# Key and value summaries of two groups of heads in one run of products, with the second group's keys and values in other buffers

## The chip, the cores and the metric

The kernel runs on one core of one Trainium2 chip. The metric is the device time of one execution in microseconds (us), as the median of several runs; lower is better. The kernel before was run three times: 836.36, 836.88 and 843.17 us.

## The reference

A small attention block feeds a gated feed-forward layer, and that feeds a layer of eight experts of which each token uses two. All of it is float32.

```python
batch, n_heads, seq, head_dim, n_mem = 4, 8, 576, 64, 32
a = exp(phi - max(phi, axis=2)); a = a / (sum(a, axis=2) + 1e-9)      # over the sequence
k_m = einsum('bhsm,bhsd->bhmd', a, k)                                 # key summary
v_m = einsum('bhsm,bhsd->bhmd', a, v)                                 # value summary
attn = softmax(q @ k_m.T / sqrt(head_dim)); x = attn @ v_m            # 2304 tokens x 512
y = (silu(x @ w_gate) * (x @ w_val)) @ w_out                          # d_ff = 1536
# experts: noisy top 2 of 8, h = relu(y @ w1[e]), out += weight * (h @ w2[e]), d_ff = 1024
```

The change touches the lines of `k_m` and `v_m` alone: for each of 4 batches and 8 heads, 32 memory rows of 64 columns, summed over 576 positions.

## The kernel before

**Stages.** The 2304 tokens are eight blocks of 288, two to a batch. The program is one list of instructions for each engine, in an order written out by hand. Stage `i` is the feed-forward layer of block `i`: 12 slots `f`, in each of which `gv(i, f)` issues 6 products into bank `pg` (line 473) and 6 into `pv`, `gate_act` makes the gated product on VectorE (DVE, lines 486 and 487), and `down` issues the output products `acc` of slot `f - 2` (line 502 in block 0, 506 later). Behind the eight stages come the experts (lines 987 to 1190).

**What is done beside a stage.** All else of the first half of the program stands at places inside the slots: `put(i, n, fn)` sets `fn` at half-slot `n` of stage `i` (n = 2f is the start of slot f, n = 2f + 1.5 lies between `gate_act` and `down`, n = 2f + 1.99 behind `down`), and `later(i, n, fn)` does so with n counted on into the next stage from 24. The table `AT["s1"]` holds these places for the summaries of batch 1 (row 1) and of batches 2 and 3 (row 2), counted from stage 2b - 2.

**The summaries.** The 8 heads of a batch are two groups `g` of 4. For a group, `s1_b` transposes the exponentials of `phi` on TensorE (PE, lines 288 to 291), `s1_bc` copies them to the tile `en`, and `s1_c` (line 310) issues 20 products into a bank `pkv`: 5 chunks of the sequence by 4 heads, each head in its own 32 columns of the array; the first 4 chunks have 128 rows, the last has 64. k and v stand side by side, so one product has 2 x 64 columns. `s1_cv` (line 319) scales the bank by the sum's reciprocal into `kz[g]` on VectorE, `s1_d` (line 328) transposes `kz[g]`, and `s1_dc` (line 336) copies the result to `KM[b]` on ScalarE (ACT). Group 1's `kz[1]` has a half of zeros (set once by GpSimd, POOL) so that its transposed rows land in the upper 64 partitions. The two groups run one behind the other, each at its own places.

**Buffers.** k and v of a batch (`load_kv`, issued by the SP queue) use one buffer `kv` for both groups in batches 1 to 3, so that group 1 is loaded only when group 0's products have read it; everything queued behind that load on SP waits with it. Three buffers of 1024 words with the tag `home` hold weights in block 0 (`stx`, from `wa`) and, at the start of the experts, the first weights `wf` and their low halves `wl`. PSUM banks 6 and 7 go round in turn to all that asks through `other`. One large store, `out<-zt`, which clears the output, is issued in stage 1 ahead of group 1's load of batch 2.

Of the kernel before, what the change touches and what calls it, by code (L numbers as in the profile page):

```python
# [7 lines left out]
F32 = mybir.dt.float32  # L8
# [4 lines left out]
I32 = mybir.dt.int32  # L13
U32 = mybir.dt.uint32
AF = mybir.ActivationFunctionType
# [5 lines left out]
B, H, S, D, M = 4, 8, 576, 64, 32  # L21
T = B * S
DM = 512
# [20 lines left out]
        7: (1.5, 4, 5, 4.05, 5.05, 6, 3, 6.05, 3.1, 3.5, 3.6, 3.7, 4, 4.01, 5.2, 6.1, 7.1, 7.2, 7.6, 7.7, 9.5, 9.6),  # L44
    },
    "s1": {
        1: (23.6, 24.02, 24.03, 25.9, 26, 26.9, 27, 27.8, 28, 27.9, 29, 31, 31.9, 33, 33.9),
        2: (9, 9.92, 13.2, 13.9, 15, 17.9, 19, 19.9, 21, 21.9, 23, 23.9, 25, 25.9, 27),
    },
# [20 lines left out]
def r(ap):  # L70
    return ap.bitcast(F32R)
# [3 lines left out]
def moe_program(ctx, tc, xin, wa, wgn, nz, wb, out):  # L75
# [10 lines left out]
    V, A, P, G, Q = nc.vector, nc.scalar, nc.tensor, nc.gpsimd, nc.sync  # L86

    const = ctx.enter_context(tc.tile_pool(name="const", bufs=1))
# [9 lines left out]
    def bank(n, shape, name):  # L98
        return psum.tile(shape, F32, tag=f"b{n}", name=name)
# [3 lines left out]
    def other(shape, name):  # L103
        spare.append(spare.pop(0))
        return bank(spare[-1], shape, name)
# [5 lines left out]
    gpool = right.enter_context(tc.tile_pool(name="gate", bufs=1, side="right"))  # L111
    att = left.enter_context(tc.tile_pool(name="att", bufs=1))


    PH, KV, QT, RA = {}, {}, {}, {}
    ROW = 18 * D

    def section(b, name):
        o, n = PLACE[name]
        return xin[b, o:o + 128 * n].rearrange("(p n) -> p n", n=n)  # L120

    def load_phi(b, g):
        t = att.tile([128, S], F32, tag="phi", name="phi", bufs=2)
        Q.dma_start(t, section(b, f"phi{g}"))
        PH[b, g] = t

    def load_part(b, g, s):
        if (b, g) not in KV:
            if b == 0 and g:
                KV[b, g] = wpool.tile([128, 4096], F32, tag="X1", name="kv", bufs=1)[:, :2 * ROW].rearrange(  # L130
                    "p (s w) -> p s w", s=2)
            else:
                KV[b, g] = att.tile([128, 2, ROW], F32, tag="kv", name="kv", bufs=1)
        Q.dma_start(KV[b, g][:, s], section(b, f"{'kv'[s]}{g}"))

    def load_kv(b, g):
        for s in range(2):
            load_part(b, g, s)
# [13 lines left out]
    for n in range(len(ORDER)):  # L152
        at, m = min((at, m) for at, m in freed if HOMES[m] is None or n < HOMES[m])
# [5 lines left out]
    def load_wa(n):  # L159


        m = HOME[n]
        if m < 4:
            RA[n] = gpool.tile([128, 1024], I32, tag="stg", name="stg", bufs=4)
        elif m < 8:
            if "x" not in RA:
                RA["x"] = wpool.tile([128, 4, 1024], I32, tag="X0", name="early", bufs=1)
            RA[n] = RA["x"][:, m - 4]
        else:
            if m not in RB:  # L170
                if m < 13:
                    RB[m] = wpool.tile([128, 1024], I32, tag="RW", name="stw", bufs=12)
                else:
                    RB[m] = gpool.tile([128, 1024], I32, tag="home", name="stx", bufs=3)
            RA[n] = RB[m]
        f, t = ORDER[n]
        Q.dma_start(RA[n].bitcast(I16)[:, :4 * DM - 1],
                    wa.bitcast(I16)[f][:, 4 * DM * t + 1:4 * DM * (t + 1)])

    RB = {}  # L180
# [4 lines left out]
    def ro_tile():  # L185
        return w1pool.tile([128, DM], F32, tag="RO", name="ro", bufs=12)
# [19 lines left out]
    def low(n):  # L206
# [5 lines left out]
        if n == 10:  # L212
            load_q(1)

    load_phi(0, 0)
    load_phi(0, 1)
    load_part(0, 0, 0)
    load_q(0)
    for g, s in ((1, 0), (0, 1), (1, 1)):
        load_part(0, g, s)  # L220
    for n in range(len(HOMES)):
# [7 lines left out]
    ident = const.tile([128, 128], F32, name="ident")  # L229
# [18 lines left out]
    e_cap = const.tile([128, E], F32, name="e_cap")  # L248
    G.iota(e_cap, pattern=[[T, E]], base=CAPS, channel_multiplier=0,
           allow_small_or_imprecise_dtypes=True)  # L250
    kz = [const.tile([128, 2, 1 + n, D], F32, name=f"kz{n}") for n in range(2)]
    G.memset(kz[1], 0.0)
    TOP = [w1pool.tile([128, 2 * DM], FP16, tag="OS", name="top", bufs=4) for _ in range(4)]
    for t in TOP:
        G.memset(t, 0.0)
# [4 lines left out]
    ST, KM = {}, {}  # L260
# [21 lines left out]
    TP = {}  # L282
# [17 lines left out]

    def s1_c(b, g, s=slice(0, 2)):

        en, st = ST[b, g]
        p = other([128, 2, D] if b else [128, D], "pkv")
        t = KV[b, g][:, s]
        for c in range(5):
            for h in range(4):
                o, d = (slice(0, 128), 4 * D * c + D * h) if c < 4 else (
                    slice(64 * (h // 2), 64 * (h // 2) + 64), 16 * D + D * (h % 2))
                P.matmul(p[32 * h:32 * h + 32], en[o, c, 32 * h:32 * h + 32], t[o, ..., d:d + D],  # L310
                         start=(c == 0), stop=(c == 4))
        TP[b, g, s if b == 0 else 2] = p

    def s1_cv(b, g, s=2, eng=None):
        st = ST[b, g][1]
        out = kz[g][:, :, g, :] if s == 2 else kz[g][:, s, g, :]
        p = TP.pop((b, g, s))
        if eng is None:
            V.tensor_scalar(out, p, st[:, 2:3], None, op0=OP.mult)
        else:  # L320
            A.activation(out, p, AF.Copy, scale=st[:, 2:3])

    def s1_d(b, g, s=2):

        p = other([128, 2, 128], "pT")
        for m in range(2):
            if s in (m, 2):
                P.transpose(p[:64 * g + 64, m, :], kz[g][:, m].rearrange("p n d -> p (n d)"), ident)
        TP[b, g, s] = p

    def s1_dc(b, g, s=2):
        if b not in KM:
            KM[b] = att.tile([128, 2, 4, M], F32, tag="km", name="km", bufs=2)
        o = slice(64 * g, 64 * g + 64)
        m = slice(0, 2) if s == 2 else slice(s, s + 1)
        A.activation(KM[b][o, m].rearrange("p s k m -> p s (k m)"), TP.pop((b, g, s))[o, m], AF.Copy)

    SM, X = {}, {}

# [105 lines left out]
    def os_tile():  # L445
        return w1pool.tile([128, DM], F32, tag="OS", name="os", bufs=4)
# [241 lines left out]
    def put(i, n, fn, *a):  # L688
        fill.setdefault((i, n), []).append((fn, a))
# [35 lines left out]
    def later(i, n, fn, *a):  # L725
        put(i + int(n // 24), n % 24, fn, *a)

    for b in range(1, B):
        i = 2 * b - 2
        n = AT["s1"][min(b, 2)]  # L730
        for g in range(2):
            later(i, 18.5 if b == 1 else -4, load_phi, b, g)
        later(i, 18.5 if b == 1 else -4, load_kv, b, 0)
        later(i, n[5] + 0.06, load_kv, b, 1)
        later(i, n[0], both, s1_a, b)
        later(i, n[1], both, s1_e, b)
        later(i, n[2], both, s1_r, b)
        for g in range(2):
            for m, fn in zip(n[3 + 6 * g:], (s1_b, s1_bc, s1_c, s1_cv, s1_d, s1_dc)):
                later(i, m, fn, b, g)  # L740
        for j, o in enumerate(AT["proj"][b]):
            i, f = 2 * b - 1 + o // NF1, o % NF1
            put(i, 2 * f + 1.95, proj_a, b, j)
            later(i, 2 * f + 2, proj_h, b, j)
            later(i, 2 * f + 2, proj_b, b, j)
    for i in range(1, NB):
        if i > 1:
            put(i - 1, 6, load_q, i)
        n = AT["s2"].get(i - 1, AT["s2"][2])
# [74 lines left out]
    WB, WH = {}, {}  # L824

    def load_wb(n):
        if n < len(STAGES) * NF2:
            if n < 2:
                WB[n] = gpool.tile([128, 1024], F32, tag="home", name="wf", bufs=3)
            elif "all" not in WB:  # L830
                WB["all"] = wpool.tile([128, 4, 1024], F32, tag="X1", name="wb", bufs=1)
            if n > 1:
                WB[n] = WB["all"][:, n % 4]
            Q.dma_start(WB[n], wb[STAGES[n // NF2], n % NF2])

    def prep2(n):
        if n % 2 == 0:
            tag = ("GH", "GL", "OS")[(n // 2) % 3]
            if n == 0:
                u = gpool.tile([128, 2, DM], F32, tag="home", name="wl", bufs=3)  # L840
                WH[n], WH[n + 1] = u[:, 0, :], u[:, 1, :]
            elif tag == "OS":
                WH[n], WH[n + 1] = os_tile(), os_tile()
            else:
                u = w1pool.tile([128, 2, DM], F32, tag=tag, name="wl", bufs=2)
                WH[n], WH[n + 1] = u[:, 0, :], u[:, 1, :]
        raw = WB[n]
        t = wpool.tile([128, 1024], F32, tag="RW", name="wm", bufs=12)
        u = ro_tile()
        A.activation(r(t), raw, AF.Copy)  # L850
        V.tensor_sub(r(u), raw[:, :512], t[:, :512])
        V.tensor_sub(r(WH[n]), raw[:, 512:], t[:, 512:])
        WB[n] = (t[:, :512], u, t[:, 512:], WH[n])
# [483 lines left out]
    for p in range(2):  # L1337
        for m in range(3):
            put(("u", (24, 25, 25, 28, 29, 29)[3 * p + m]), 1.2, sums_ws, p, m)
        for n in range(4):  # L1340
            u = (25, 26, 27, 27, 29, 30, 30, 31)[4 * p + n]
# [11 lines left out]
    for p in range(pairs):  # L1353
        e, q = 2 + p // 4, p % 4
        n = 24 + 2 * p
# [138 lines left out]
    with tc.If(full > 0), tc.tile_pool(name="last", bufs=1) as last:  # L1494
        w = last.tile([128, NF2, 1024], F32, name="wl")
# [58 lines left out]
```

## Time and profile before

| | |
|---|---|
| median of 3 runs | 836.88 us |
| the profiled execution, whole | 836.54 us |
| its span, first to last instruction | 834.7 us |
| PE busy | 820.9 us |
| DVE busy | 637.0 us |
| ACT busy | 391.8 us |
| POOL busy | 244.7 us |
| mean granted TensorE clock | 0.998 |

The profiled execution lies between the runs: 0.34 us under their median. The span leaves out 1.8 us around the first and the last instruction. Busy times overlap; PE's is nearly the span, but its matmuls are pipelined, so what one of them costs is read from the start of one group to the start of the next, not from its own duration.

### The profile page before, as it was taken

Reading aid. Unit: us, or ns where it says so; the run is one execution under the profiler, and the core shown is the slowest. Engines: PE = TensorE matmul, PEld = TensorE weight load, DVE = VectorE, ACT = ScalarE, POOL = GpSimd, SP = SyncE. Lnnn points to the kernel's source line nnn. Section 1 sums busy time; section 2 is a strip of 40 time slices with the busy share of each in tenths; the row PEclk is TensorE's granted clock in tenths of the full one; section 3 lists DMA queues with packets and bytes.
Section 4 is the critical chain, followed back from the end, with each engine's and each line's share of the span. In section 5 each row is a group of like instructions: output and inputs, shape, how many; then the busy total and the mean of one; then the engine's idle time right before and its main releaser. Section 6 shows DMA issues by size and latency. Waiting matters only on the chain.

```text
span 834.7 us, 16643 instructions
## 1 busy us (share of the span) xinstructions
PE 820.9 (98%) x6317; PEld 730.7 (88%) x6317; DVE 637.0 (76%) x1534; ACT 391.8 (47%) x804; POOL 244.7 (29%) x345
## 2 busy tenths in 40 slices
PE   7999999999999999999999999999999999999996
PEld 5777988999899998999999988888888888888885
DVE  5887688776867677868684597898889988899761
ACT  5765565343443334333444555555455454554430
POOL 2000012424233252453122233123315233145132
PEclk9999999999999999999999999999999999999999
DMA  9993649775426373448747973555465644654421
GB/s 350 400 397 122 204 161 327 234 247 142 116 67 216 84 212 96 120 127 217 233 160 217 237 202 91 127 144 128 101 166 131 144 128 94 161 143 111 159 84 65
DMA packets 79145, 143.20 MB, mean 172 GB/s; under 512 B 16176, under 2 KB 36880, under 8 KB 79056
## 3 DMA queue, kind: packets, MB, share of 16 engines
q1 hardware_dynamic: 59696, 100.66, 38.4%
q0 software_dynamic: 19360, 41.38, 20.5%
q8 instruction: 52, 0.85, 0.4%
q14 instruction: 37, 0.30, 0.1%
HBM read 105.34 MB, written 36.68 MB: 170 GB/s over the span
## 4 chain that ended last, share of the span: by engine, by line
PE 89%; DMA 7%; DVE 2%; issue 1%; ACT 1%; SPq 0%; POOL 0%; POOLq 0%; DVEq 0%; ACTq 0%
PE acc L1190 18%; PE ph L1176 17%; PE acc L506 16%; PE pg L473 9%; PE pv L473 8%; PE acc L1005 7%; PE ph L987 7%; PE pp L346 2%; DMA out<-pv,ix 1%; DMA early<-wa 1%; DMA stw<-wa 1%; PE pT L528 1%; DMA stx<-wa 1%; DMA stg<-wa 1%; PE pkv L310 1%; DMA qt<-xin 1%
## 5 line engine op out<-in xcount | busy, mean ns | idle before, releaser
L1190 PE MATMUL acc<-ws,hs 128*128 128x512 f32 (+1 forms) x690 | 174.9, 394 | 0.0
L1176 PEld LDWEIGHTS ph<-xh,ws 128*128 128x128 f32 x1008 | 150.9, 188 | 9.7 <-ACT y L1213 0.7
L1176 PE MATMUL ph<-xh,ws 128*128 128x308 f32 x1008 | 157.4, 304 | 0.3 <-ACT y L1213 0.3
L1190 PEld LDWEIGHTS acc<-ws,hs 128*128 128x128 f32 (+1 forms) x690 | 122.7, 184 | 24.3
L506 PE MATMUL acc<-a,ro 128*128 128x288 f32 x576 | 116.4, 295 | 0.0
L1030 POOL DMA_INDIRECT out<-pv,ix x40 | 63.0, 1575 | 177.8 <-ACT pv L1022 67.5
L506 PE MATMUL acc<-a,os 128*128 128x288 f32 x432 | 106.0, 295 | 0.0
L473 PE MATMUL pg<-x,pt 128*128 128x288 f32 x576 | 101.3, 310 | 0.7 <-DVE a L486 0.2
L473 PEld LDWEIGHTS pg<-x,pt 128*128 128x128 f32 x576 | 81.0, 188 | 18.3 <-issue 6.4
L506 PEld LDWEIGHTS acc<-a,ro 128*128 128x128 f32 x576 | 92.1, 188 | 0.0
L473 PE MATMUL pv<-x,pt 128*128 128x288 f32 x576 | 91.9, 295 | 0.0
L473 PEld LDWEIGHTS pv<-x,pt 128*128 128x128 f32 x576 | 81.7, 188 | 0.0
L670 POOL DMA_INDIRECT xs<-R,gidx x48 | 48.1, 1003 | 111.5 <-DMA xs<-R,gidx 93.6
L486 DVE SCALAR_TENSOR_TENSOR ta<-ta,pg 128x288 f32<-128x288 f32 x84 | 37.6, 448 | 55.0 <-ACT ta L481 54.9
L506 PEld LDWEIGHTS acc<-a,os 128*128 128x128 f32 x432 | 74.1, 189 | 0.3 <-ACT ro L459 0.2
L481 ACT ACTIVATE ta<-pg 128x288 f32<-128x288 f32 x84 | 34.4, 410 | 82.2 <-PE pg L473 82.1
L492 ACT ACTIVATE a<-ta 128x288 fp32r<-128x288 f32 x84 | 37.3, 444 | 68.9 <-DVE ta L487 68.8
L463 POOL DMA_DIRECT2D os<-osl x72 | 40.8, 567 | 97.3 <-PE acc L506 56.0
L987 PE MATMUL ph<-xt,wm 128*128 128x384 f32 (+1 forms) x256 | 55.4, 307 | 0.0
L987 PEld LDWEIGHTS ph<-xt,wm 128*128 128x128 f32 x256 | 43.7, 189 | 2.6
L487 DVE TENSOR_TENSOR ta<-ta,pv 128x288 f32<-128x288 f32 x84 | 38.1, 454 | 8.8
L493 DVE TENSOR_TENSOR a<-ta,a 128x288 fp32r<-128x288 f32 x84 | 37.5, 447 | 5.8 <-ACT a L492 5.6
(241 smaller groups left out, 1448.1 us busy)
## 6 DMA issues: line engine op xcount, KB each, us to landing
wb<-wb SPq DMA_DIRECT2D x70, 512.0 KB, 4.4
os<-osl POOLq DMA_DIRECT2D x72, 256.0 KB, 3.4
kv<-xin SPq DMA_DIRECT2D x16, 576.0 KB, 6.5
xl<-xs SPq DMA_DIRECT2D x40, 160.0 KB, 6.7
stg<-wa SPq DMA_DIRECT2D x12, 511.8 KB, 10.2
out<-zt SPq DMA_DIRECT2D x1, 5888.0 KB, 24.7
xd<-R SPq DMA_DIRECT2D x8, 603.0 KB, 5.6
qt<-xin SPq DMA_DIRECT2D x8, 576.0 KB, 6.9
```

The lines of the kernel that those rows point to most:

```text
L463: G.dma_start(r(lo), r(osl[f][:, :]))
L473: P.matmul(p, r(PT[f // 2, g][:, w, f % 2, 128 * a:128 * a + 128]), r(X[i][:, s, g, :]), start=(n == 0), stop=(n == 5))
L486: V.scalar_tensor_tensor(ta, ta, 1.0, pg, op0=OP.add, op1=OP.mult)
L487: V.tensor_mul(ta, ta, pv)
L493: V.tensor_sub(r(ah[:, 1, :]), ta, ah[:, 0, :])
L506: P.matmul(ACC[i][c], r(OS[i, f][w][:, o]), r(ah[:, s, :]), start=(f == 0 and n == 0), stop=(f == NF1 - 1 and n == 2))
L670: G.indirect_dma_start(out=xs[:, :], out_offset=bass.IndirectOffsetOnAxis(ap=RT[i][:, t, n:n + 1], axis=0), in_=R[i][:, t, :], in_offset=None)
L987: P.matmul(p, r(w[:, c]), r(x[:, k, b, :]), start=(m == 0), stop=(m == 11))
L1005: P.matmul(AC2[e, t][:h], r(a[:, o:o + h]), r(b), start=(f == 0 and m == 0), stop=(f == NF2 - 1 and m == 2))
L1030: G.indirect_dma_start(out=out, out_offset=bass.IndirectOffsetOnAxis(ap=IX[e][:h, t:t + 1], axis=0), in_=PV[e, t][:h], in_offset=None, com ...
L1176: P.matmul(out, r(w[i][:, c + 128 * k:c + 128 * k + 128]), r(x[:, m, k, a]), start=(start and n == 0), stop=(n == 5), skip_group_check=not ...
L1190: P.matmul(AC2[e, t][:h], r(a[:, n, o]), r(w[b][:, n]), start=(f == 0 and m == 0), stop=(f == NF2 - 1 and m == 2))
```

## The change

In batches 1 to 3 the products of both groups are issued in one run, `s1_cc`, into one bank: group 0 with chunks 0 to 4, then group 1 with chunk 4 first and then 0 to 3, so that the two 64-row chunks stand side by side. Two `s1_cv` follow, then one pair of transposes of a single tile `kz` that holds both groups (`s1_dd`, instead of a pair for each), and one copy of 128 x 256 (`s1_ddc`, instead of two of 64 x 256). The half of zeros and its memset go. Batch 0 keeps its own steps, on the single `kz`.

Group 1's k and v get a buffer of their own, the tag `home`, which becomes one tile of 2304 words in place of three of 1024. In block 0 its two parts hold two of the three `stx` weights, and a new tag `wl` of 1024 words holds the third; at the experts they hold the two `wf`, and `wl` the low halves. Both groups' loads are now issued together. The places in `AT["s1"]` are drawn together: 15 become 11.

```diff
     "s1": {
-        1: (23.6, 24.02, 24.03, 25.9, 26, 26.9, 27, 27.8, 28, 27.9, 29, 31, 31.9, 33, 33.9),
-        2: (9, 9.92, 13.2, 13.9, 15, 17.9, 19, 19.9, 21, 21.9, 23, 23.9, 25, 25.9, 27),
+        1: (23.6, 24.02, 24.03, 25.9, 26, 27.9, 29, 31, 31.9, 33, 33.9),
+        2: (9, 9.92, 13.2, 13.9, 15, 17.9, 19, 19.9, 21, 21.9, 23),
...
+    def home():
+        return gpool.tile([128, 2 * ROW], F32, tag="home", name="home", bufs=1)
...
+            elif g:
+                KV[b, g] = home().rearrange("p (s w) -> p s w", s=2)
...
+    def s1_cc(b):
+        p = other([128, 2, 2, D], "pkv")
+        for g, chunks in enumerate(((0, 1, 2, 3, 4), (4, 0, 1, 2, 3))):
+            s1_m(b, g, slice(0, 2), p[:, g], chunks)
+            TP[b, g, 2] = p[:, g]
...
+    def s1_dd(b):
+        p = TP[b, "d"] = other([128, 2, 128], "pT")
+        for m in range(2):
+            P.transpose(p[:, m], kz[:, m].rearrange("p n d -> p (n d)"), ident)
+
+    def s1_ddc(b):
+        KM[b] = att.tile([128, 2, 4, M], F32, tag="km", name="km", bufs=2)
+        A.activation(KM[b].rearrange("p s k m -> p s (k m)"), TP.pop((b, "d")), AF.Copy)
...
-        later(i, n[5] + 0.06, load_kv, b, 1)
+        later(i, 23.99 if b == 1 else -4, load_kv, b, 1)
...
-            for m, fn in zip(n[3 + 6 * g:], (s1_b, s1_bc, s1_c, s1_cv, s1_d, s1_dc)):
-                later(i, m, fn, b, g)
+            later(i, n[3 + 2 * g], s1_b, b, g)
+            later(i, n[4 + 2 * g], s1_bc, b, g)
+        later(i, n[7], s1_cc, b)
+        later(i, n[8], both, s1_cv, b)
+        later(i, n[9], s1_dd, b)
+        later(i, n[10], s1_ddc, b)
```

On PE, where block 0 ends and stage 1 begins (batch 1), before: group 0's products `pkv`, its transposes of `kz`, and group 1's transposes of `phi`.

```order
L473 MATMUL pv<-x,pt 128x288 x6
L310 MATMUL pkv<-kv,en 32x128 x20
L502 MATMUL acc<-a_1016,ro 128x288 x4
L328 MATMUL pT<-ident,kz_156 64x128 x2
L288 MATMUL pT<-ident,phi 128x128 x4
L290 MATMUL pT<-ident,phi 128x128
L291 MATMUL pT<-ident,phi 64x128
L473 MATMUL pg<-x,pt 128x288 x6
```

And from the same `acc` on, after the change (lines are those of the changed kernel):

```order
L525 MATMUL acc<-a_1013,ro 128x288 x4
L296 MATMUL pT<-ident,phi 128x128 x4
L298 MATMUL pT<-ident,phi 128x128
L299 MATMUL pT<-ident,phi 64x128
L496 MATMUL pg<-x,pt 128x288 x6
L496 MATMUL pv<-x,pt 128x288 x6
L529 MATMUL acc<-a_1042,os 128x288 x12
L551 MATMUL pT<-ident,gx 96x128 x4
L496 MATMUL pg<-x,pt 128x288 x6
L496 MATMUL pv<-x,pt 128x288 x6
L322 MATMUL pkv<-kv,en 32x128 x20
L322 MATMUL pkv<-home,en 32x128 x20
```

Group 0's 20 products moved two slots back, to stand ahead of group 1's 20, and one pair of transposes is gone.

On DVE, in stage 2 (batch 2), before: the copy of group 0's bank to `kz_156` behind the gated product (`ta`), ahead of the softmax of a later block (`rd`, `sm`).

```order
L486 SCALAR_TENSOR_TENSOR ta<-ta,pg 128x288
L487 TENSOR_TENSOR ta<-ta,pv 128x288
L319 TENSOR_SCALAR kz_156<-pkv,st 128x128
L379 TENSOR_REDUCE rd<-sm 128x9
L380 TENSOR_SCALAR rd<-rd 128x9
L381 RECIPROCAL rd<-rd 128x9
```

And after, one slot later:

```order
L509 SCALAR_TENSOR_TENSOR ta<-ta,pg 128x288
L510 TENSOR_TENSOR ta<-ta,pv 128x288
L336 TENSOR_SCALAR kz<-pkv,st 128x2x64 x2
L427 TENSOR_TENSOR x<-at,x 128x288
L402 TENSOR_REDUCE rd<-sm 128x9
```

Both copies now stand together, right behind the gated product of slot 10.

On the SP queue, from the end of stage 1 on, before: the large store, group 1's load of batch 2, and what is queued behind it.

```order
L142 DMA qt<-xin 128x1152
L714 DMA out<-zt 128x23x512
L134 DMA kv<-xin 128x1152 x2
L675 DMA xd<-R 96x3x536
L142 DMA qt<-xin 128x1152
```

And after, from the load of batch 2 on:

```order
L139 DMA kv<-xin 128x1152 x2
L139 DMA home<-xin 128x1152 x2
L477 DMA osl_80<-os 128x512
L477 DMA osl_81<-os 128x512
L477 DMA osl_82<-os 128x512
L147 DMA qt<-xin 128x1152
L737 DMA out<-zt 128x23x512
L698 DMA xd<-R 96x3x536
L147 DMA qt<-xin 128x1152
```

Group 1's load moved ahead of the large store, and the store `xd<-R` and the load `qt` now follow the large store directly.

## Rows read from the trace of the kernel before

**Rows 1.** The page, busy time by engine: busy us (share of the span) xinstructions.
```profile
PE 820.9 (98%) x6317; PEld 730.7 (88%) x6317; DVE 637.0 (76%) x1534; ACT 391.8 (47%) x804; POOL 244.7 (29%) x345
```
**Rows 2.** Busy time by stretch: stretch, length, engines busy (xcount), clock, DMA share, GB/s.
```profile
145.00:150.00 5.00, 5.00 (x50) 4.38 (x49) 3.19 (x14) 1.21 (x5) 3.24 (x12) 1.00 1.06 404
145.00:180.00 35.00, 35.00 (x383) 32.06 (x381) 25.33 (x87) 12.64 (x34) 14.52 (x29) 1.00 0.83 278
```
**Rows 3.** Waits of PE, 60 to 280 us: total us, times, longest.
```profile
PE pp L346 <- DVE wa L208: 0.3, 1, 0.3
PE pg L473 <- DVE a L486: 0.2, 1, 0.2
PE pg L473 <- DVE pt L443: 0.2, 1, 0.2
```
**Rows 4.** Timeline of PE, two plain slots: start us, us, line, operation, count.
```profile
208.16 0.96 PE L473 MATMUL pv<-x,pt 128*128 128x288 f32 x6
...
211.35 0.96 PE L473 MATMUL pv<-x,pt 128*128 128x288 f32 x6
```
**Rows 5.** Timeline of PE, batch 2, group 0: products and transposes.
```profile
156.58 0.95 PE L473 MATMUL pv<-x,pt 128*128 128x288 f32 x6
...
159.05 1.43 PE L310 MATMUL pkv<-kv,en 128*32 128x128 f32 x40
160.41 1.06 PE L473 MATMUL pg<-x,pt 128*128 128x288 f32 x6
161.31 0.95 PE L473 MATMUL pv<-x,pt 128*128 128x288 f32 x6
...
163.69 0.38 PE L328 MATMUL pT<-ident,kz 128*64 128x128 f32 x2
...
164.71 0.96 PE L473 MATMUL pv<-x,pt 128*128 128x288 f32 x6
```
**Rows 6.** The end of that run, two narrow stretches: earliest start still running, us, count.
```profile
159.84 0.53 PE L310 MATMUL pkv<-kv,en 128*32 128x128 f32 x7
160.06 0.42 PE L310 MATMUL pkv<-kv,en 64*32 64x128 f32 x8
```
**Rows 7.** Timeline of PE, batch 1: three `pv` at the end of block 0.
```profile
71.95 0.96 PE L473 MATMUL pv<-x,pt 128*128 128x288 f32 x6
...
76.14 0.96 PE L473 MATMUL pv<-x,pt 128*128 128x288 f32 x6
...
82.36 0.95 PE L473 MATMUL pv<-x,pt 128*128 128x288 f32 x6
```
**Rows 8.** Timeline of DVE in the slot behind that run (batch 2).
```profile
162.95 0.34 DVE L319 TENSOR_SCALAR kz<-pkv,st 128x128 f32<-128x128 f32 x1
163.21 0.44 DVE L379 TENSOR_REDUCE rd<-sm 128x9 f32<-128x288 f32 x1
```
**Rows 9.** Timelines of POOL and of the SP queue.
```profile
145.28 0.59 POOL L463 DMA_DIRECT2D os<-osl  x1 [0.23 <-issue]
146.59 0.23 POOL L659 TENSOR_TENSOR R<-R 96x24 f32<-96x24 f32 x1 [0.72 <-DVE goh L662]
...
78.53 0.81 SPq L134 DMA_DIRECT2D kv<-xin  x2
...
161.45 0.38 SPq L675 DMA_DIRECT2D xd<-R  x1
```
**Rows 10.** DMA issues, KB each, us to landing; PE's first use of the first.
```profile
os<-osl POOLq DMA_DIRECT2D x1, 256.0 KB, 6.4
...
xd<-R SPq DMA_DIRECT2D x8, 603.0 KB, 5.6
...
qt<-xin SPq DMA_DIRECT2D x8, 576.0 KB, 6.9
...
157.63 0.29 PE L506 MATMUL acc<-a,os 128*128 128x288 f32 x1
```
**Rows 11.** Timeline of DVE, the end of block 0: a late read of a `stx` weight.
```profile
69.42 0.68 DVE L208 SCALAR_TENSOR_TENSOR ro<-stx,top 128x512 int32<-128x512 int32 x1
```

More of the change, by code (lines that the diff above doesn't have):

```diff
@@ L173, in load_wa @@
                 else:
-                    RB[m] = gpool.tile([128, 1024], I32, tag="home", name="stx", bufs=3)
+                    if "home" not in RB:
+                        RB["home"] = home().bitcast(I32)
+                        RB[15] = gpool.tile([128, 1024], I32, tag="wl", name="stx", bufs=1)
+                    if m < 15:
+                        RB[m] = RB["home"][:, 1024 * (m - 13):1024 * (m - 12)]
             RA[n] = RB[m]
@@ L250, in moe_program @@
            allow_small_or_imprecise_dtypes=True)
-    kz = [const.tile([128, 2, 1 + n, D], F32, name=f"kz{n}") for n in range(2)]
-    G.memset(kz[1], 0.0)
+    kz = const.tile([128, 2, 2, D], F32, name="kz")
     TOP = [w1pool.tile([128, 2 * DM], FP16, tag="OS", name="top", bufs=4) for _ in range(4)]
@@ L301, in s1_c, with s1_m @@
     def s1_c(b, g, s=slice(0, 2)):
+        p = other([128, D], "pkv")
+        s1_m(b, g, s, p, range(5))
+        TP[b, g, s] = p
+    def s1_m(b, g, s, p, chunks):
         en, st = ST[b, g]
-        p = other([128, 2, D] if b else [128, D], "pkv")
         t = KV[b, g][:, s]
-        for c in range(5):
+        for n, c in enumerate(chunks):
             for h in range(4):
@@ L310, in s1_c @@
                 P.matmul(p[32 * h:32 * h + 32], en[o, c, 32 * h:32 * h + 32], t[o, ..., d:d + D],
-                         start=(c == 0), stop=(c == 4))
-        TP[b, g, s if b == 0 else 2] = p
+                         start=(n == 0), stop=(n == 4))
+    def s1_cc(b):
[3 more added lines that the diff above has]
+            TP[b, g, 2] = p[:, g]
     def s1_cv(b, g, s=2, eng=None):
         st = ST[b, g][1]
-        out = kz[g][:, :, g, :] if s == 2 else kz[g][:, s, g, :]
+        out = kz[:, :, g, :] if s == 2 else kz[:, s, g, :]
         p = TP.pop((b, g, s))
@@ L321, in s1_cv, with s1_d, s1_dc @@
             A.activation(out, p, AF.Copy, scale=st[:, 2:3])
[L323 to L328, printed above, removed]
+    def s1_d(b, g, s):
+        p = other([128, 128], "pT")
+        P.transpose(p[:64 * g + 64], kz[:, s, :g + 1].rearrange("p n d -> p (n d)"), ident)
         TP[b, g, s] = p
-    def s1_dc(b, g, s=2):
+    def s1_dc(b, g, s):
         if b not in KM:
@@ L334, in s1_dc @@
         o = slice(64 * g, 64 * g + 64)
-        m = slice(0, 2) if s == 2 else slice(s, s + 1)
-        A.activation(KM[b][o, m].rearrange("p s k m -> p s (k m)"), TP.pop((b, g, s))[o, m], AF.Copy)
+        A.activation(KM[b][o, s].rearrange("p k m -> p (k m)"), TP.pop((b, g, s))[o], AF.Copy)
+    def s1_dd(b):
[5 more added lines that the diff above has]
+        A.activation(KM[b].rearrange("p s k m -> p s (k m)"), TP.pop((b, "d")), AF.Copy)
     SM, X = {}, {}
@@ L828, in load_wb @@
             if n < 2:
-                WB[n] = gpool.tile([128, 1024], F32, tag="home", name="wf", bufs=3)
+                if n == 0:
+                    WB["home"] = home()
+                WB[n] = WB["home"][:, 1024 * n:1024 * n + 1024]
             elif "all" not in WB:
@@ L839, in prep2 @@
             if n == 0:
-                u = gpool.tile([128, 2, DM], F32, tag="home", name="wl", bufs=3)
+                u = gpool.tile([128, 2, DM], F32, tag="wl", name="wl", bufs=1)
                 WH[n], WH[n + 1] = u[:, 0, :], u[:, 1, :]
```

## The prediction

> **What bounds the kernel now.** I read the page first: PE is busy for 820.9 of 834.7 us, DVE for 637.0 [rows 1]. A busy PE need not be a PE at its peak, so next comes the table by stretch, for the stages that the change touches. Between 145 and 180 us, which holds batch 2's summaries, PE is busy for 35.00 of 35.00 us at a granted clock of 1.00, which is the 2.4 GHz level [rows 2]. The list of PE's waits from 60 to 280 us has three rows, 0.7 us in all [rows 3]. So in these stages PE is the bound, it waits for next to nothing, and what is taken from its queue should come off the time one for one. The other engines matter only where they come to be late for PE.
>
> Since PE's matmuls overlap, I take prices from the timeline, as distances between the starts of equal groups. A slot with nothing put into it is 211.35 - 208.16 = 3.19 us from one `pv` to the next [rows 4]. What a slot with an insertion has above 3.19 us is the price of the insertion, with its drains and all.
>
> **The products of one group.** Batch 2, group 0: from the `pv` at 156.58 to the `pv` at 161.31 is 4.73 us, with the 40 records of `pkv` between (20 products, two records each). So one run costs 4.73 - 3.19 = 1.54 us [rows 4, 5]. Batch 2's other run and batch 3's two look alike in the timeline.
>
> What is in the 1.54 us? The records start four at a time, one for each head's 32 columns. The first four start at 159.05 and the eighth four at 159.84: 0.79 us for 7 steps, 0.113 us a step [rows 5, 6]. The ninth four, the first of 64 rows, come 0.22 us later, at 160.06, so the switch of shape from 128 to 64 rows costs some 0.11 us above a step [rows 6]. Ten steps are 1.13 us; the other 0.41 us are the way in, the switch, and the way out to the next `pg`.
>
> **The joined run** saves one way in, one way out and one of two switches, and adds a switch back from 64 to 128 rows, which nothing in the trace shows. Its second half costs ten steps, 1.13 us, at least. At most it costs what a run by itself does, 1.54 us. I take the switch back at the price of the switch there, as the nearest row: 1.13 + 0.11 = 1.24 us.
>
> The page "TensorEngine Tiling" of the Trainium skill (Key Properties) says that a change of tiling mode drains TensorE, while another tile in the same mode does not. The 0.22 us step at the change of rows agrees with it [rows 6]. By the rule the joined run has four changes where two runs had six, which is the sum above; it also speaks against the change in one point, since the switch back is a new one.
>
> **The transposes of `kz`.** Group 0's pair goes. From the `pv` at 161.31 to that at 164.71 is 3.40 us, with only this pair put in: 0.21 us [rows 4, 5]. Group 1's pair stays, and now carries both groups.
>
> **Batch by batch.**
> - Batch 2: 1.54 + 0.21 - 1.24 = 0.51 us off.
> - Batch 3 has the same places and the same rows in its stage: 0.51 us.
> - Batch 1: group 0's products, its transposes of `kz` and group 1's transposes of `phi` stand in one stretch of block 0's end, from the `pv` at 76.14 to that at 82.36, 6.22 us. The stretch ahead of it, from the `pv` at 71.95 to that at 76.14, holds all that is left of it after the change: a `pv`, an `acc` of block 0, the transposes of `phi` (there group 0's) and a `pg`. It takes 4.19 us [rows 7]. That gives 2.03 us off, more than 1.54 + 0.21, because the transposes of `phi` are also held up a little behind those of `kz`. Less the joined half: 2.03 - 1.24 = 0.79 us.
>
> The sum is 0.51 + 0.51 + 0.79 = 1.81 us. With the joined half at 1.54 us it is 0.21 + 0.21 + 0.49 = 0.91; with it at 1.13 us it is 2.14.
>
> **What costs nothing, and its cover.** ACT's two copies to `KM` become one, DVE's two copies of `pkv` stay two: both engines have idle time in these stages (DVE 25.33, ACT 12.64 of 35.00 us) [rows 2]. The memset of zeros on POOL was one instruction of the prologue; its going is counted at nothing. In block 0 the order and the waits of the weights' loads stay as they are; only where they lie changes. The load of group 1 of batch 1 now waits for the last read of the two `home` weights; the third last weight is read at 69.42 us, by 70.1 that is over [rows 11]. SP holds the stores of `xs` behind it until then, but before it held most of them longer, until group 0's products had been read and the load went out at 78.53 us [rows 9]. The joined run of batch 1 stands where group 1's products stood, behind the `pv` at 82.36 us, which comes 2.03 us sooner now, so the load has more than 10 us to land [rows 7]. Its bytes are the same, so the DMA engines move as much as before, only sooner.
>
> **The rivals.**
>
> *The second copy is late.* In batches 2 and 3 the transposes now wait for two copies instead of one. In the slot behind group 0's run the copy starts 162.95 - 160.41 = 2.54 us after `pg`, the next DVE instruction 0.26 us later; a second copy of 0.34 us would end 3.14 us after `pg`. PE came to the transposes at 163.69, 3.28 us after `pg` [rows 5, 8]. That leaves 0.14 us. If DVE is late by a whole copy in both batches, 2 x 0.34 = 0.68 us are given back: 835.4 us. For it speaks the thin margin; against it, that `pg` waits for nothing there and DVE has less to do in the slot before.
>
> Beside this stands a sentence of the same page of the Trainium skill (PSUM Bottleneck): tiling speeds up TensorE but not the emptying of PSUM, and the copy may become the bottleneck. The trace has the copy 0.14 us ahead so far, which is not yet that case.
>
> *The joined run is no cheaper than two.* If the way into and out of a run is really paid per group (a new wait on the loads and on `en` stands at the 21st product), the half costs 1.54 us and 0.91 us remain: 835.6 us. Against it: between equal shapes the steps are even, 0.113 us [rows 5, 6].
>
> *Slower: the down weights come late.* Before, SP sat on group 1's load of batch 2 until PE had read the buffer, and issued the store `xd<-R` at 161.45 only, though POOL had `R` ready at 146.6 [rows 9]. Now SP goes on at once, and this store (603 KB) and the load `qt` behind it (576 KB) fall into the large clearing store, where the DMA engines already run at 1.06 of their share and 404 GB/s [rows 2, 10]. POOL's load at 145.28 landed after 6.4 us, and PE first used it at 157.63, 12.35 us after issue [rows 9, 10]. The moved bytes at 404 GB/s are 2.9 us, which fits into the slack of 5.9. Only if the load took over 12.35 + 1.81 = 14.2 us would the kernel be slower than before. At 16 us, two and a half times its landing, PE would wait 3.65 us and the time would be 836.54 - 1.81 + 3.65 = 838.4 us. I see nothing that would slow it so.
>
> *The change doesn't do what it says* would show as two runs that stand apart. The written order has them side by side, so this is left with no chance of its own.
>
> **How the numbers follow.** The sum is made against the profiled execution: 836.54 - 1.81 = 834.7 us. The median of the runs lies 0.34 us above that execution, which would give 835.1. I take the middle, 834.9 us.
>
> Chances: my forecast 0.72, a late copy 0.12, no cheaper than two 0.09, late weights 0.05, others 0.02. The low end is the largest saving, 836.54 - 2.14 = 834.4, less a microsecond for the spread of the runs: 833.3. The high end is the slower rival with 838.4; it takes in both smaller savings and the case of none at all, at 836.9. One of three runs of before lay at 843.2, so the spread is wider upward.
>
> A measurement of this kernel can tell about 1% from no change, 8.4 us. No case above reaches that downward; upward only a weight load far later than reckoned would. So: faster 0.02, same 0.95, slower 0.03.
>
> **What would show it.** In the profile after: one run of 80 `pkv` records in each of batches 1 to 3, with `pv` to `pv` around it at 3.19 + 1.54 + 1.24 = 5.97 us where nothing else is put in. At the change from group 0 to group 1 the shape stays 64 rows, and a step of some 0.22 us follows where the rows go back to 128. The slot with the pair of `kz` transposes at about 3.4 us in batches 2 and 3; a longer one is the late copy. PE's waits between 60 and 280 us still under 1 us, and PE busy about 1.8 us less over the page. `xd<-R` issued near 147 us. I would be wrong if the second half of the run costs 1.5 us, if a wait for DVE or for `os` shows up ahead of `pT` or `acc`, or if the stages behind batch 3 don't start about 1.8 us earlier than before.

## The result and the profile after

| | before | after |
|---|---|---|
| median of the runs | 837.20 us (6 runs) | 842.85 us (6 runs, 842.49 to 844.19) |
| profiled execution, span | 836.54, 834.7 us | 843.15, 841.3 us |
| granted clock, mean | 0.998 | 0.994 |

The ratio of the runs is 1.0057, with a 95% interval of 1.0037 to 1.0077 (the two medians alone give 1.0067): the change makes the kernel 0.6% slower. The forecast was 834.9 us with a range up to 838.4, so the time lies outside the range, on the other side of before. Within 1% of before, which was given 0.95, is right. Two runs of far longer time, 1334.5 us of the kernel with one idle buffer below and 2825.6 us of the one before beside it, are left out of the medians and ratios below.

The page has PE busier than before [rows 1], not less busy. That suggests that something slowed PE down rather than only made it wait:

```profile
span 841.3 us, 16623 instructions
...
PE 824.6 (98%) x6311; PEld 735.1 (87%) x6311; DVE 636.1 (76%) x1534; ACT 391.3 (47%) x801; POOL 242.7 (29%) x344
```

To find the place I laid the starts of `pv`, one per slot, of both traces side by side. The difference is constant over long stretches and jumps in a few slots:

| `pv` before | `pv` after | shift | step there |
|---|---|---|---|
| 82.36 | 80.36 | -2.00 | -2.03 (group 0's run and transposes of batch 1 gone) |
| 91.15 | 90.41 | -0.74 | +1.26 (second half of the joined run) |
| 132.05 | 131.30 | -0.75 | |
| 136.10 | 142.07 | +5.97 | **+6.72** |
| 161.31 | 166.58 | +5.27 | -0.89 (batch 2) |
| 164.71 | 172.58 | +7.87 | +2.60 |
| 168.57 | 176.01 | +7.44 | -0.43 |
| 173.30 | 179.62 | +6.32 | -1.12 |
| 176.71 | 182.80 | +6.09 | -0.23; the five of batch 2 sum to -0.07 |

Batch 3 repeats batch 2: -0.90, +2.61, -0.40, -1.16, -0.22, in sum -0.07. So there are two surprises: 6.72 us in one slot, the third of block 2, and some 0.44 us less than forecast in each of the batches 2 and 3.

**The large one.** PE's waits from 60 to 280 us, which had three rows of 0.2 to 0.3 us before [rows 3], have a new first row:

```profile
PE acc L529 <- DMA os<-osl: 3.8, 1, 3.8
PE pp L369 <- DVE wa L217: 0.3, 1, 0.3
PE pg L496 <- DVE a L509: 0.2, 1, 0.2
PE pg L496 <- DVE pt L466: 0.2, 1, 0.2
```

The timeline of PE has it in the slot of the jump. `acc` is the down product of block 2's first slot, `os` the low half of its weight, which POOL reads back from `osl`:

```profile
131.30 0.95 PE L496 MATMUL pv<-x,pt 128*128 128x288 f32 x6
132.09 0.42 PE L529 MATMUL acc<-a,ro 128*128 128x288 f32 x2
136.36 0.61 PE L529 MATMUL acc<-a,os 128*128 128x288 f32 x1 [3.85 <-DMA os<-osl]
...
140.49 1.79 PE L496 MATMUL pg<-x,pt 128*128 128x288 f32 x6
142.07 1.15 PE L496 MATMUL pv<-x,pt 128*128 128x288 f32 x6
```

The wait is 3.85 us. The rest lies behind it: from the product that waited to the next `pv` it is 142.07 - 136.36 = 5.71 us. Before, the same work took 136.10 - 133.11 = 2.99 us. The stretches show why (stretch, length, engines busy, then the granted clock, DMA share and GB/s). After:

```profile
132.00:136.00 4.00, 0.51 (x4) 0.28 (x3) 3.18 (x15) 0.44 (x1) 0.10 (x1) 0.96 1.09 393
136.00:140.00 4.00, 3.64 (x16) 3.55 (x17) 0.00 (x0) 0.00 (x0) 0.53 (x1) 0.50 1.14 383
140.00:144.00 4.00, 4.00 (x24) 3.98 (x23) 1.08 (x4) 1.03 (x3) 0.00 (x0) 0.69 1.05 404
144.00:148.00 4.00, 4.00 (x35) 3.35 (x34) 1.73 (x7) 1.56 (x5) 0.53 (x1) 1.00 1.08 400
```

PE, which had been busy all along, stood still in the first of these stretches. The granted clock then fell to 0.50, the 1.2 GHz level, and came back to 1.00 by the fourth; in stretches of 1 us it is 0.50 from 136 to 142 us. Before, all four show 4.00 us busy at 1.00. So the jump of 6.72 us is two things. The first product with `os` starts 5.06 us behind its `pv` instead of 1.06, which makes 4.00 us, of which the list calls 3.85 a wait. The other 5.71 - 2.99 = 2.72 us are slow work behind it.

**Why the data came late.** The timeline of the SP queue and of POOL, after:

```profile
115.99 0.85 SPq L139 DMA_DIRECT2D kv<-xin  x2
116.94 1.08 SPq L139 DMA_DIRECT2D home<-xin  x2
118.11 8.94 SPq L477 DMA_DIRECT2D osl<-os  x3
127.14 0.38 SPq L147 DMA_DIRECT2D qt<-xin  x1
127.58 0.44 SPq L737 DMA_DIRECT2D out<-zt  x1
...
129.00 1.90 POOL L486 DMA_DIRECT2D os<-osl  x3 [19.77 <-PE acc L529]
```

and before:

```profile
116.75 0.85 SPq L134 DMA_DIRECT2D kv<-xin  x2
117.70 10.10 SPq L454 DMA_DIRECT2D osl<-os  x3
127.90 0.39 SPq L142 DMA_DIRECT2D qt<-xin  x1
128.34 0.48 SPq L714 DMA_DIRECT2D out<-zt  x1
...
126.28 1.44 POOL L463 DMA_DIRECT2D os<-osl  x2 [16.29 <-ACT a L492]
```

The two loads of `home` for batch 2 now stand right ahead of the last three stores of `osl`, those of slots 9 to 11 of stage 1. POOL's loads of `os` for block 2 reuse the four buffers that hold the high and low halves of these slots' weights, and the stores read the low halves. As the changed program is built, the first of these loads gets the buffer of slot 9's low half, and has to wait until the store of slot 9 has landed. The timeline names PE's `acc` as what ended the wait, but the landing events in the trace fit the store better: it lands at 128.38 us, and the load goes out 0.62 us later. In the other runs that use this buffer so the distance is 0.61 or 0.62 us again (0.54 in the run with two idle buffers), while that to PE's last event varies from 0.03 to 0.34.

Before, the first load got the buffer of slot 10's high half, which no store reads. It went out 0.59 us behind PE's last product with that half, whose end the trace has at 125.69 us; the store of slot 9 landed at 125.94.

So POOL's first loads went out at 129.00 us instead of 126.28: behind the clearing store `out<-zt` (5888 KB, issued at 127.58), no longer ahead of it (128.34). Beside that store the first took 136.36 - 129.00 = 7.4 us to be of use. In the kernel before, the two ahead of the store landed 3.2 and 4.1 us after issue, and the third, behind it, after 8.3. This order of events is a reading of the traces; the runs below test it.

"DMA: Bandwidth & Descriptors" of the Trainium skill (Queues, rings and completion order) says that each DMA engine takes packets in turn from the queues that have work. The trace agrees: POOL's load was slowed to 7.4 us by SP's store, but did not wait for its end, which is 24.7 us from issue in the trace of before.

### The profile page after: what moved, and what is told of

Its sections match the earlier page's. It is cut to its first block, busy times and chain, and to the rows that moved or that the text cites. A ratio compares the mean times of both kernels' runs of the same rounds, so it can differ in the third digit from the quotient of the medians.

```text
span 841.3 us, 16623 instructions
## 1 busy us (share of the span) xinstructions
PE 824.6 (98%) x6311; PEld 735.1 (87%) x6311; DVE 636.1 (76%) x1534; ACT 391.3 (47%) x801; POOL 242.7 (29%) x344
## 4 chain that ended last, share of the span: by engine, by line
PE 86%; DVE 6%; DMA 5%; issue 1%; ACT 1%; POOL 0%; POOLq 0%; DVEq 0%; ACTq 0%
PE acc L1219 18%; PE ph L1205 17%; PE acc L529 14%; PE pg L496 9%; PE pv L496 7%; PE ph L1016 7%; PE acc L1034 7%; PE pp L369 2%; PE acc L525 1%; DMA out<-pv,ix 1%; PE pT L551 1%; DMA home<-wa 1%; DMA osl<-os 1%; PE pkv L322 1%; DVE wa L217 1%
```

## The experiments

Theory A is that reading; B blames the joined run or the rest of the new order; C blames the bytes of `home` wherever they go. All ratios are to the kernel before, run on the same chip in the same round, with 95% intervals.

### Batch 2's loads behind the clearing store

```diff
-        later(i, 23.99 if b == 1 else -4, load_kv, b, 1)
+        later(i, {1: 23.99, 2: 8.01, 3: -4}[b], load_kv, b, 1)
```

> Batch 2's two loads into home stand behind the clearing store in SP's queue instead of ahead of the stores of os; the rest is the changed kernel. Theory A (the loads put ahead of the stores of os make POOL's first loads of os start behind the clearing store, PE waits 3.85 us for them and then runs some us at half clock): PE's wait for os at the start of block 2 goes, the granted clock stays at 1.00 from 132 to 144 us, and the time is about 836.3 us, some 0.9 us under before (0.75 from batch 1, 0.07 from each of the others). Theory B (the joined run, or the rest of the new order, brings the loss): it stays at 842 to 843 us. Theory C (home's bytes slow whatever runs beside them, wherever they stand): a wait of 1 us or more for os or home shows up somewhere between 130 and 165 us.

Measured: 836.35 us, ratio 0.9982 (0.9966 to 0.9998). No wait of PE between 60 and 280 us is over 0.2 us. The clock is 1.00 in every stretch from 112 to 184 us, POOL's first loads go out at 126.28 us, and the jump of 6.72 us is gone. The steps of -2.03, +1.27 and those of batches 2 and 3 are as in the changed kernel. Theory A holds, B falls, and C has no wait to show.

### Batch 2's loads between the last `osl` store and the clearing store

```diff
-        later(i, 23.99 if b == 1 else -4, load_kv, b, 1)
+        later(i, {1: 23.99, 2: 4.01, 3: -4}[b], load_kv, b, 1)
```

> Batch 2's two loads into home stand behind the last store of os and ahead of the clearing store. Theory A: the stores of os land as before, POOL's first two loads of os go out near 125.5 us, and PE waits for nothing at 132.5 us: about 836.3 us, like the run with the loads behind the clearing store. Theory C: the loads of os run beside 1152 KB of home and land late, PE waits 1 us or more and the time is above 838 us.

Measured: 837.39 us, ratio 1.0000 (0.9976 to 1.0024). The trace is as expected by A: POOL's first loads at 126.57 us, no wait over 0.2 us, no jump, although `home` moves right beside these loads. C falls. The time is 1 us over what was expected, and the interval leaves room for both; this median proves no gain. In this run and in the one above POOL's first load also has its buffer of before (slot 10's high half), so these two change the place of the loads and the choice of the buffer together.

### The early loads alone, with two runs as before

The joined run is taken apart into two runs with their own copies and transposes, at the places of the kernel before. The buffers and the loads stay as in the changed kernel.

```diff
-        later(i, n[7], s1_cc, b)
-        later(i, n[8], both, s1_cv, b)
-        later(i, n[9], s1_dd, b)
-        later(i, n[10], s1_ddc, b)
+            for m, fn in zip(n[3 + 6 * g:], (s1_b, s1_bc, s1_c2, s1_cv, s1_d2, s1_dc2)):
+                later(i, m, fn, b, g)
```

> The loads of group 1 early, into home, as in the changed kernel, but two separate runs of products, copies and transposes at the places of the kernel before. Theory A: the same wait for os near 132.5 us, 3.8 us long, with the low clock behind it, and none of the savings: 843 to 844 us. Theory B: no wait, 837 us, as before.

Measured: 843.77 us, ratio 1.0065 (1.0039 to 1.0090). The whole loss is there without the joined run:

```profile
136.24 0.61 PE L544 MATMUL acc<-a,os 128*128 128x288 f32 x1 [3.28 <-DMA os<-osl]
```

The step in that slot is 6.16 us, the clock falls to 0.50 again, and all other slots keep their times of before to 0.5 us. So the moved loads carry the loss, and the joined run has no part in it.

### The clearing store later

The clearing store stands at half-slot 8 of stage 2 (above it is said to be issued in stage 1; SP issues it at 128.34 us, ahead of PE, which is in the second slot of stage 2). Here it goes to the end of that stage.

```diff
-    put(2, 8, init_out)
+    put(2, 23.99, init_out)
```

> The changed kernel with the clearing store put behind the first store of R in SP's queue (some 20 us later); the loads into home stay ahead of the stores of os. Theory A: POOL still issues its first loads of os near 129.0 us, but nothing large is ahead of them, so they land some 3.7 us later, near 132.7, and PE, which comes to them near 132.5, waits 0.5 us at most; the time is 836.3 to 837 us. If the late issue alone were the cause (Theory D: the loads into home still fill the queues), the wait stays at 2 us or more and the time above 840 us. Theory B: 842 to 843 us.

Measured: 842.38 us, ratio 1.0049 (1.0028 to 1.0070). The time is a miss, but the place expected came out as A said: POOL issues at 128.24 us, and the first product with `os` starts at 132.06, with no wait listed. So the late issue does no harm without the clearing store ahead. The loss came back 40 us later:

```profile
176.74 0.61 PE L529 MATMUL acc<-a,os 128*128 128x288 f32 x1 [3.01 <-DMA os<-osl]
```

The step there is 4.83 us and the next slot adds 0.80, again with the clock at 0.50 behind the wait. POOL's timeline tells why:

```profile
151.62 0.58 POOL L486 DMA_DIRECT2D os<-osl  x1
159.56 0.95 POOL L693 DMA_INDIRECT xs<-R,gidx  x1 [7.36 <-DMA xs<-R,gidx]
160.51 0.56 POOL L486 DMA_DIRECT2D os<-osl  x1
167.94 0.96 POOL L693 DMA_INDIRECT xs<-R,gidx  x1 [6.87 <-DMA xs<-R,gidx]
168.89 0.56 POOL L486 DMA_DIRECT2D os<-osl  x1
```

Each scatter of rows waits for the one before to land. Beside the clearing store, now issued at 146.30 us, that takes some 7 us. The loads of `os` are queued behind the scatters and fall behind PE. In the kernel before, the first scatter goes out at 151.49 us, 1.5 us before the clearing store has landed.

### One idle buffer

The loads stay early. Only the first load of `os` of block 2 goes into a buffer that nobody uses at that time (`wl`, last used in block 0), so it waits for no `osl` store but its own.

```diff
-        lo = os_tile()
+        if (i, f) == (2, 0):
+            lo = gpool.tile([128, 1024], F32, tag="wl", name="os", bufs=1)[:, :DM]
+        else:
+            lo = os_tile()
```

> The changed kernel with the loads early, ahead of the stores of os, as it has them; only the first load of os of block 2 goes into a buffer that lies idle at that time (4 KB of wl) instead of one whose last store must land. Theory A: POOL issues this load near 109 us, long before the clearing store, PE does not wait for it, and the second load, issued near 129 us and landing near 136.3, is used at 136.3: a wait of 0 to 0.5 us, and 836.3 to 837 us. If the traffic of home by itself held PE up, the wait and the 843 us would stay.

Measured: 836.58 us, ratio 0.9982 (0.9962 to 1.0002). The wait and the jump are gone:

```profile
110.15 0.80 POOL L489 DMA_DIRECT2D os<-osl  x1
129.12 1.10 POOL L489 DMA_DIRECT2D os<-osl  x2 [18.17 <-DMA osl<-os]
```

The second load now has the buffer of slot 9's low half. The store of slot 9 lands as late as in the changed kernel, at 128.50 us, and the load goes out 0.62 us behind it, at 129.12; here the trace names an `osl` store as the releaser, where in the changed kernel it named PE. With the first load free of that buffer, PE has no wait. So the late landing by itself costs nothing: it has to hold the load that PE needs next.

### The wait filled with work

```diff
+        if n - 2 == 2 * NF1:
+            p = other([128, BT], "spin")
+            for _ in range(30):
+                P.matmul(p, r(RO[0][:, :128]), r(ACT1[2, 0][0][:, 0, :]), start=True, stop=True)
         down(*divmod(n - 2, NF1))
```

> The changed kernel, with 30 products into an unused bank ahead of the down product that waits for os at the start of block 2. They take about 30 x 0.133 = 4.0 us and end near 136.1 us, so the wait of 3.85 us is filled with work that nobody reads. If the 6.9 us are a wait of 3.85 us and some 3 us of half clock behind it, the wait row goes, the granted clock stays at 1.00 from 132 to 144 us, the slot still costs 4.0 us, and the time is about 3 us under that of the changed kernel: near 840 us. If the 3 us behind the wait have another cause (late data of the rest of the slot), the time stays near 843 us.

> The filled wait again, with 28 products in two banks instead of 30 in one. With one bank every later user of the two spare banks changed places, and the last stage came 2 us later at its end, though the slot at the start of block 2 had grown by 4.86 us instead of 6.72. With two banks the places stay as they are. If that swap was what hid the gain: the granted clock stays at 1.00 from 132 to 144 us, the slot grows by 4.7 to 4.9 us, and the time is 1.9 us under that of the changed kernel, about 841 us or a ratio of 1.0035 to before. If the clock is not what the 1.9 us are, or the end is late for another reason, 843 us or more.

The second run issues 14 products into each of two banks. In the slot the first came out as expected: 0.23 us of the wait are left. In the second 1.03 us are left, more than expected. In neither does the clock fall; the stretches of the first:

```profile
132.00:136.00 4.00, 3.86 (x30) 3.62 (x29) 3.36 (x15) 0.58 (x2) 0.38 (x1) 1.00 1.08 389
136.00:140.00 4.00, 3.77 (x30) 3.52 (x30) 0.00 (x0) 0.00 (x0) 0.53 (x1) 1.00 1.14 378
140.00:144.00 4.00, 4.00 (x36) 3.35 (x34) 2.31 (x8) 1.54 (x4) 0.53 (x1) 1.00 1.06 404
```

From the first product with `os` to the next `pv` the first run takes 140.38 - 137.28 = 3.10 us, near the 2.99 of before, not 5.71. The slot grows by 4.86 us in the first and 5.38 in the second, where 4.7 to 4.9 was expected, and by 6.72 in the changed kernel. So the slow work behind the wait is the clock.

The whole time is a miss in both: 844.99 and 844.38 us, ratios 1.0079 (1.0055 to 1.0103) and 1.0071 (1.0044 to 1.0098). The changed kernel ran again beside the second:

> The changed kernel again, on the same chip and beside the same runs of before as the filled wait, for the comparison of the two: 842.9 us, a ratio of 1.0057.

It gave 843.74 us, 1.0062 (1.0044 to 1.0080), so the gain of the slot is not in the time. In both profiles it is lost at the end. PE's last product ends at 831.8 and 832.8 us, against 834.2 in the changed kernel, but the last five scatters into `out` spread over 17.1 to 17.2 us, against 836.38 - 821.58 = 14.8. Keeping the order of the two spare banks, in the second of the runs, did not change that. Why these scatters take longer is open, and so is why the first run's median lies 1.9 us above its profiled execution.

### The joined run as cover

In batches 2 and 3 the joined run, its copies and transposes move to the places where group 1's stood before, at the end of the block. One run has it on top of the loads behind the clearing store. The other has it on the kernel as changed, with the first two loads of `os` in the idle buffer.

```diff
-        2: (9, 9.92, 13.2, 13.9, 15, 17.9, 19, 19.9, 21, 21.9, 23),
+        2: (9, 9.92, 13.2, 13.9, 15, 17.9, 19, 23.9, 25, 25.9, 27),
```

> The run with batch 2's loads behind the clearing store, and in batches 2 and 3 the joined run, its copies and transposes at the places where group 1's stood before. If the 0.43 us that each of these batches lost was the chain of the next block's softmax, which group 1's run had covered: pg to pv at the two borders 0.9 us or less instead of 1.24, and about 0.86 us less than the run without this move, 835.4 us. If not, 836.3 us as that run.

> As the run before, but the first two loads of os of block 2 go into the idle buffer, and in batches 2 and 3 the joined run, its copies and transposes stand where group 1's products stood before (at the end of the block, ahead of the next block's first gate products). Theory A and the theory that the chain of the softmax is now uncovered there: no wait for os at all, pg to pv at the two borders 0.9 us or less instead of 1.24, some 0.4 us back in each of the batches, and 835.3 to 835.8 us. If the removed 0.4 us were not the uncovered chain, 836.3 us.

Measured: 835.68 us, ratio 0.9978 (0.9956 to 0.9999), and 835.56 us, ratio 0.9968 (0.9953 to 0.9984). What the move cures stands in the changed kernel's timelines at the border of batch 3's block, DVE first, then PE:

```profile
273.91 0.45 DVE L509 SCALAR_TENSOR_TENSOR ta<-ta,pg 128x288 f32<-128x288 f32 x1 [0.47 <-ACT ta L504]
274.46 0.45 DVE L510 TENSOR_TENSOR ta<-ta,pv 128x288 f32<-128x288 f32 x1
274.84 0.45 DVE L427 TENSOR_TENSOR x<-at,x 128x288 fp32r<-128x288 f32 x1
...
274.47 1.40 PE L496 MATMUL pg<-x,pt 128*128 128x288 f32 x6
275.72 0.96 PE L496 MATMUL pv<-x,pt 128*128 128x288 f32 x6
```

`pg` of the new block needs both parts of its `x`. DVE writes the last part at 274.84 to 275.29 us, after `pg` has begun, so `pg` takes 1.25 us to `pv`, where 0.80 to 0.90 is usual. It is a stop between two of its six products, which no list of waits shows, for PE's group of six counts as one. Before, group 1's run stood ahead of this `pg` and covered DVE, whose last part of `x` was done at 266.98 us, 1.04 us ahead of `pg`:

```profile
266.48 0.50 DVE L404 TENSOR_TENSOR x<-at,x 128x288 fp32r<-128x288 f32 x1
...
266.66 1.43 PE L310 MATMUL pkv<-kv,en 128*32 128x128 f32 x40
268.02 1.06 PE L473 MATMUL pg<-x,pt 128*128 128x288 f32 x6
268.93 0.96 PE L473 MATMUL pv<-x,pt 128*128 128x288 f32 x6
```

With the joined run moved there, as in the run with two idle buffers (batch 2):

```profile
172.98 1.05 PE L501 MATMUL pg<-x,pt 128*128 128x288 f32 x6
173.88 0.96 PE L501 MATMUL pv<-x,pt 128*128 128x288 f32 x6
```

0.90 us, and the steps of batch 2 are -0.89, -0.19, -0.69 and +1.23: -0.54 us in place of -0.07. Batch 3 gives -0.56. Against the two runs without the move, the medians fall by 0.67 and 1.02 us, where 0.86 was expected. These differences lie within the intervals of the ratios, the first pair was not run side by side, and the second also has one more load in the idle buffer; the first 60 us alone differ by up to 2.3 us between the profiled executions. So the steps carry this reading, not the medians. The last two kernels are faster than both before and after, by 0.2 and 0.3%: the intervals end at 0.9999 and, for the one with two idle buffers, at 0.9984.

## Why the prediction was wrong, by its steps

- **What bounds the kernel now**: right. PE waited for next to nothing, and what was taken off or put on its queue came off or on.
- **The joined run**: right. The second half was taken at 1.24 us and cost 1.26. In batch 2 the slot of the run is 172.58 - 166.58 = 6.00 us, forecast 5.97. The switch back from 64 to 128 rows, which was guessed from the switch there, takes a step of 0.22 us in the trace (170.45 to 170.67), as that one does. The page "TensorEngine Tiling (Array Packing)" of the Trainium skill (Key Properties) says that a change of tiling mode drains TensorE. The trace agrees: 0.22 us at either change of rows, against 0.11 between equal shapes.
- **Batch 1**: right, -2.03 and +1.26 make -0.77 us, forecast -0.79.
- **The transposes of `kz` and the late second copy**: the slot is 176.01 - 172.58 = 3.43 us, forecast about 3.4, so that rival did not come.
- **Batches 2 and 3**: the terms were right, a cover was missed. The prediction asked what hides the copies and what is late next for the transposes. It did not ask what group 1's run, which was taken from its place, had itself been hiding. It stood ahead of the next block's first `pg` and covered DVE's last part of `x`. Of 0.51 us a batch 0.07 was left; with the cover restored 0.54 and 0.56.
- **The step that failed**: "What costs nothing, and its cover", with "Its bytes are the same, so the DMA engines move as much as before, only sooner". It followed batch 1's load to its use and counted batch 2's at nothing. In batch 2 "sooner" means ahead of three stores in SP's queue, whose landing POOL's loads need, just before the largest transfer of the stage; and the new order gave the first of these loads a buffer that waits for the first of the stores. The runs price it at 6.72 us: 4.00 by which PE came late to its first product with `os`, and 2.72 behind it at the lower clock.
- **The slower rival** had the right kind of mechanism, weights of down that come late, and the right neighbour, the clearing store. It looked for it at the load issued at 145.28 us, with slack 5.9 us [rows 9, 10], and not at the first loads of the block, which before went out 2 us ahead of that store. It also took the wait alone as the price and left out the clock. Its chance of 0.05 was too low and its time too short.
- **Small slips**: 834.4 less a microsecond is 833.4, not 833.3, and the 1179 KB of the slower rival at 404 GB/s are 3.0 us, not 2.9, since the page counts 1024 bytes to a KB. Nothing hangs on either.

The chain of causes is shown at both ends: the early loads alone bring the loss, and loads behind the `osl` stores, or one free buffer for POOL's first load, take it away. In between, two things came together. The stores land later, and POOL's first load goes into the buffer of a low half, which such a store reads; before it went into that of a high half, which none does. The buffer pools choose that as the program is built, and the choice changed with the order of the loads. The run with the idle buffer shows that the late landing costs nothing when the first load is free of it. The other half, the new choice with the stores landing as early as before, was not run. An estimate from the traces: the store of slot 9 landed at 125.94 us then, and 0.62 us behind it the load would have gone out at 126.56, only 0.28 us later than it did.

## What to carry to other kernels

A load moved earlier is not free because its bytes are the same: go through its queue from the new place to the old one, and for each transfer that it is now ahead of, ask which buffer is waiting for it, and what large transfer is about to start. Look at which buffers the built program hands out, too: a new order of loads can change that where no line of the source does. When work is taken out of the queue of the engine that sets the time, ask what that work was covering, at its old place and not only at its new one. And price a wait of that engine with what the clock does afterwards: here a delay of 4.00 us cost 6.72.

## What the runs showed of the hardware

- One stop of 3.85 us on PE, after more than 60 us of nearly unbroken work, brought the granted clock down to 0.50, where it stood from 136 to 142 us. Stops of 3.28 and 3.01 us in two of the runs did the same. With the stop filled with products that nobody reads, 0.23 and 1.03 us of it were left and the clock stayed at 1.00.
- A load of 256 KB from POOL took 7.4 us to be of use beside a store of 5888 KB on SP's queue, against 3.2 and 4.1 us to landing for two such loads ahead of that store in the kernel before. POOL's scatters, each waiting for the last to land, held it idle for 7.36 and 6.87 us beside the store, against 1.55 and 1.59 for the first two such waits in the kernel before, where the store had landed (later ones there, beside other transfers, took up to 5.75).
- In both kernels with the filled wait the last five scatters took 2.3 us longer in all than in the changed kernel, though their stage has the same instructions. This stays open.
